# RetNet retention and a gated feed-forward: group 3 begun inside the first block, weights' exponents one part ahead

## The chip, the cores and the metric

One core of a Trainium2 chip runs the whole kernel. The metric is the device time of one execution in microseconds (us); lower is better. The engines named below are PE (TensorE, matrix products), DVE (VectorE), ACT (ScalarE), POOL (GpSimd, here mostly a queue of DMAs) and SP (SyncE, a queue of DMAs). Each engine runs its own instructions in the order in which the program gives them; PE's weight loads run beside its matmuls.

## The reference, cut to what matters

```python
# q, k, v: (4, 8, 768, 64) float32; w_in (512, 2048) and w_out (2048, 512) arrive as float64
for t in range(S):                                   # retention, per batch and head
    state = gamma * state + outer(k[:, :, t], v[:, :, t])
    y[:, :, t] = q[:, :, t] @ state / 8
x = y.transpose(0, 2, 1, 3).reshape(3072, 512)
h = x @ w_in                                         # "hidden"
g = h * erf(softplus(h))
out = (g @ w_out).astype(float32)                    # "project"
```

## The kernel before

**Tokens.** The 3072 tokens are 24 chunks of 128. Chunks 2g and 2g+1 form group g of 256 tokens, so there are 12 groups. Retention is computed chunk by chunk: queries and keys are transposed (`ret_transpose`, or `prepare` with DVE's transposes from chunk 6 on), `begin` makes scores and state updates on PE, `states` masks the scores and adds up the state on DVE, `results` makes the outputs on PE, and `crossed_sums` adds two halves on DVE. The outputs of a group stand in `XC[g]`.

**Weights.** The eight pieces of `w_in` (n = 0 to 7, two of the 16 column tiles `ft` each, 1 MB as float64) are loaded by SP (`load_piece`, L175) and turned into float32 by hand (`conversion`, L204). DVE takes the exponent bits (L216), ACT scales them (L219), and DVE makes the mantissa (L223, L228), puts the sign to the scaled exponent (L230) and multiplies (L242). Pieces 0 to 3 are converted in two half-width parts, the others whole. The call of L219 stands directly behind L216 of the same part, so L230 needs an ACT result that was asked for two or three DVE instructions before. `need("in", ft)` runs conversion steps until tile `ft` is ready. The eight pieces of `w_out` follow later through POOL (`load_quarter`, `convert`).

**First block.** Groups 0 and 1 (the first 512 tokens) meet `w_in` in plain float32: 16 steps, one for each `ft`, each 16 PE instructions (`hidden_of`, L642) and one eviction by ACT (`put_hidden`, L650) into a tile of two that `ps_h` has. The table `during` says what else is put in after which `ft`: before, the whole retention of group 2 (chunks 4 and 5) stands at ft 5 to 13, the loads of chunks 6 and 7 (`load_pair`, the generator `pair`; 32 DMAs of 32 KB in four steps and then four of 256 KB) at ft 6 to 10, and the first splits of weights at ft 8 to 15.

**Periods.** From group 2 on, weights and tokens are split into three fp32r parts (`split_weights`, `split_x`), and a product is three fp32r products. There are two forms of work. A unit alone (`unit`, L667) takes two column tiles for one group: 24 matmuls of 256 columns. A unit in pairs (`pair_unit`, L709) takes one column tile for two groups: 12 matmuls of 512 columns. `period(g)` lists eight or fewer units, puts `begin` and `results` of the next group's chunks between them (`joined`), and the DVE and ACT work beside them. One unit alone of group 2 (n = 7) runs in plain float32 (L679), since its weights aren't split yet. Before, 18 units are alone: eight of group 2, five of group 3, one of group 4 and four of group 11. `put` evicts a unit's two accumulators with one ACT and one DVE instruction (`together`, L296 and L297) and stores the hidden values to DRAM.

**End.** After the periods the hidden values are read back, gated and projected (`project`, L889).

Of the kernel before, what the change touches and what calls it, by code (L numbers as in the profile page):

```python
# [13 lines left out]
F32 = mybir.dt.float32  # L14
# [35 lines left out]
def kernel(  # L50
# [24 lines left out]
    FIRST = 4  # L75
# [25 lines left out]
    HID = {g: scratch.tile([P, n_ft, GT], F32, name=f"hid{g}") for g in (*range(FIRST + 1), NG - 1)}  # L101
# [72 lines left out]
    def load_piece(n, part=None):  # L174

        if n not in RAW:
            if n % 4 < 2:
                RAW[n] = b8("raw", [2 * d_model], I64)
            else:
                raw = ring.tile([P, 3 * d_model], I64, name="raw", tag=f"x{n % 4 - 2}")  # L180
                RAW[n] = raw[:, : 2 * d_model]
        f = slice(2 * P) if part is None else slice(part * P, (part + 1) * P)
        each = 1 if part is None else 2
        for g in range(0, n_k, each):
            nc.sync.dma_start(
                RAW[n].rearrange("p (g f) -> p g f", g=n_k)[:, g : g + each, f],
                w_in[g * P : (g + each) * P, n * 2 * P : (n + 1) * 2 * P].rearrange(
                    "(g p) f -> p g f", p=P
                )[:, :, f],
            )  # L190
# [11 lines left out]
    behind = []  # L202

    def conversion(n):  # L204

        WF[n] = b4("w", [2, 2, 2 * P])
        POWER[n] = b4("power", [2, 2, 2 * P])
        for part in range(2) if n < 4 else (None,):  # L210
            f = slice(2 * P) if part is None else slice(part * P, (part + 1) * P)
            words = RAW[n].bitcast(U32).rearrange("p (h a b w) -> p h a b w", h=2, a=2, w=2)[:, :, :, f]
            to, power = WF[n][..., f], POWER[n][..., f].bitcast(U32)
            number = to.bitcast(U32)
            lo, hi = words[..., 0], words[..., 1]
            nc.vector.tensor_scalar(power, hi, 0x7FF00000, None, op0=ALU.bitwise_and)  # L216
            exponent = partial(nc.scalar.activation, power, power, AF.Relu, bias=below, scale=8.0)
            if n < NPC:
                exponent()  # L219
            else:  # L220
                behind.append(exponent)
            yield
            nc.vector.tensor_scalar(  # L223
                number, hi, 0xFFFFF, 1 << 20, op0=ALU.bitwise_and, op1=ALU.bitwise_or
            )
            if part is None:
                yield
            nc.vector.scalar_tensor_tensor(to, number, 2.0**32, lo, op0=ALU.mult, op1=ALU.add)  # L228
            yield
            nc.vector.scalar_tensor_tensor(  # L230
                power, hi, 1 << 31, power, op0=ALU.bitwise_and, op1=ALU.bitwise_or
            )
            if part != 0:
                del RAW[n]
                if n + 4 < NPC:
                    load_piece(n + 4)
                if n < 2:
                    load(JPC + n)
                    load_values(JPC + n)
            if part is None:  # L240
                yield
            nc.vector.scalar_tensor_tensor(  # L242
                to, to, 2.0**-52, power.bitcast(F32), op0=ALU.mult, op1=ALU.mult,
            )
            if n < NPC:
                done.update(("in", 2 * n + u) for u in (range(2) if part is None else (part,)))
            else:
                nc.gpsimd.dma_start(
                    WOF[n - NPC],
                    WF.pop(n).rearrange("p h a f -> p (h a f)").rearrange("p (f c) -> p f c", f=2),  # L250
                )
            yield

    def weights():


        for n in range(2 * NPC):
            yield from conversion(n)
# [275 lines left out]
    def begin(j, pool=ps_h):  # L534

        SC[j] = [ret_psum(pool) for _ in range(2)]
# [80 lines left out]
    def split_x(j, n=1):  # L617
        g, i = divmod(j, 2)
        if i == 0:
            if g == JPC // 2:  # L620
                X[g] = [b4(f"x_{x}", [HP, GT], F32R) for x in ("hi", "lo", "dif")]
            else:
                if not XR:
                    XR.extend(
                        ring.tile([P, 3, HP, GT], F32R, name=f"x_{x}", tag=f"x{i}")
                        for i, x in enumerate(("hi", "lo", "dif"))
                    )
                X[g] = [x[:, g % 3] for x in XR]
# [27 lines left out]

    def unit(g, n):

        if n in W:
            pool = next(last_turn) if g == NG - 1 else ps_o  # L660
            own = next(turn) if pool is ps_o else None
            names = [f"o{2 * own + i}" if pool is ps_o else "hp" if pool is ps_h else "r" for i in range(2)]
            a, b = (pool.tile([P, 2, GT], F32, name=name) for name in names)
            for to, parts in ((a, (0, 1)), (b, (2,))):
                for u in range(2):
                    for kk, i in itertools.product(range(n_k), parts):
                        nc.tensor.matmul(  # L667
                            to[:, u],
                            W[n][i][:, kk * 2 * P + u * P : kk * 2 * P + (u + 1) * P],
                            X[g][i][:, kk],  # L670
                            start=(u == 0 and kk == 0 and i == parts[0]),
                            stop=(kk == n_k - 1 and i == parts[-1]),
                            skip_group_check=True,
                        )
        else:
            a, b = ps_o.tile([P, 2, GT], F32, name=f"o{2 * next(turn)}"), None
            w = WF[n].rearrange("p h a f -> p (h a) f")
            for u, kk in itertools.product(range(2), range(n_k)):
                nc.tensor.matmul(  # L679
                    a[:, u], w[:, kk, u * P : (u + 1) * P], XC[g][:, kk],  # L680
                    start=(u == 0 and kk == 0), stop=(kk == n_k - 1), skip_group_check=True,
                )

        def put():
            h = b2("h", [2, GT])
            if b is None:
                nc.scalar.copy(h, a)
            else:
                together(h, a, b)
# [8 lines left out]
    def pair_unit(g, ft):  # L698

        pool = next(last_turn) if g == NG - 2 else ps_o  # L700
        own = next(turn) if pool is ps_o else None
        names = [f"o{2 * own + i}" if pool is ps_o else "hp" if pool is ps_h else "r" for i in range(2)]
        a, b = (pool.tile([P, 2, GT], F32, name=name) for name in names)
# [13 lines left out]
        def put():  # L717
            h = b2("h", [2, GT])
            together(h, a, b)
            if g < FIRST:  # L720
                for of in (g, g + 1):
                    nc.gpsimd.dma_start(HID[of][:, ft], h[:, place_of(g, of)])
            else:
                nc.gpsimd.dma_start(HID2[g][:, ft % 8], h)  # L724
# [52 lines left out]

    def steps(s, n=1):
# [8 lines left out]
        5: [(Q_, a), (V_, a)],  # L787
        6: [(T, a, None, ("o2", "o3")), (steps, pair, 2)],
        7: [(begin, a, ps_r), (steps, pair, 2)],
        8: [(states, a), (Q_, b), (V_, b), (split_weights, 0), (steps, pair, 2)],  # L790
        9: [(results, a, ("o0", "o1")), (T, b, None, ("o2", "o3")), (steps, pair, 2)],
        10: [(crossed_sums, a), (begin, b, ps_r), (steps, pair), (block_scales,)],
        11: [(states, b), (split_x, a)],
        12: [(results, b, ("o0", "o1"))],
        13: [(crossed_sums, b), (split_x, b), (split_weights, 1)],
        14: [(split_weights, 2), (steps, prep, 2)],
        15: [(split_weights, 3), (steps, prep, 3)],
    }
    for ft in range(n_ft):
# [4 lines left out]
        need("in", min(ft + 2, n_ft - 1))  # L804
# [9 lines left out]
    def load_hidden(n):  # L814
# [5 lines left out]
        of = g if g % 2 == i // 2 else g - 1  # L820
# [95 lines left out]

    def period(g, prep, next_prep):
# [3 lines left out]
        if g == G2:  # L921
            units = [one(g, n) for n in (0, 7, 1, 2, 3, 4, 5, 6)]
            return units, joined(3, 5, g), {
                1: [(split_weights, 4)],
                2: [(split_weights, 5)],
                3: [(states, a), (states, b)],
                4: [(split_weights, 6)],
# [3 lines left out]
            }, range(8)  # L931
        if g == G2 + 1:
            units = [one(g, n) for n in range(5)]
            return units, joined(1, 3, g), {
                0: [(steps, prep)],
                1: [(states, a), (states, b)],
                2: [(split_weights, 7)],
                3: [(crossed_sums, a), (crossed_sums, b), (split_x, a, 2)],
# [141 lines left out]
```

## Time and profile before

| | |
|---|---|
| median of 3 runs | 617.8 us (616.19 to 619.2) |
| the profiled execution's own time | 616.22 us |
| its span, first to last instruction | 614.4 us |
| PE busy | 606.4 us, 99% |
| DVE, ACT, POOL busy | 461.1, 379.1, 104.2 us |
| granted TensorE clock | 1.000 |
| chain that ended last | PE 96% |

The profiled execution is one of the shorter ones: it lies 1.6 us under the median. Start times below are microseconds from the start of the span.

### The profile page before, as it was taken

What the parts mean: (1) busy time and instruction counts of PE and PEld (TensorE: products, weight loads), DVE (VectorE), ACT (ScalarE), POOL (GpSimd) and SP (SyncE); (2) the same over time, 40 slices, a digit from 0 to 9 for tenths busy, and PEclk for the clock granted to TensorE, in tenths of its full rate; (3) what the DMA queues carried; (4) which work ended last, traced back from release to release, by engine and by line L of the source; (5) the groups of instructions that cost most, each with busy time, mean ns of one, the idle gap of its engine ahead of it and who ended that gap; (6) DMA issues with size and microseconds to landing.
All of it is one profiled execution on the core that took longest, in us unless ns stands there. A gap on an engine that the chain in (4) does not pass through costs nothing.

```text
span 614.4 us, 13336 instructions
## 1 busy us (share of the span) xinstructions
PE 606.4 (99%) x5334; PEld 514.0 (84%) x5334; DVE 461.1 (75%) x583; ACT 379.1 (62%) x566; POOL 104.2 (17%) x198
## 2 busy tenths in 40 slices
PE   8999999999999999999999999999999999999997
PEld 7888899998888888888888988888888888888885
DVE  5988897786878779798758978686786768668640
ACT  3333473563544535454487699879789888988910
POOL 1085332213333242321111200000000000000000
PEclk9999999999999999999999999999999999999999
DMA  9999659677889899787645834325324333531301
GB/s 202 326 249 278 150 130 259 172 160 191 234 238 243 217 264 264 211 231 203 231 136 192 302 118 126 133 84 172 103 83 157 104 127 112 171 123 49 104 34 35
DMA packets 175022, 106.29 MB, mean 173 GB/s; under 512 B 140016, under 2 KB 155632, under 8 KB 174960
## 3 DMA queue, kind: packets, MB, share of 16 engines
q1 hardware_dynamic: 162016, 67.53, 43.3%
q0 software_dynamic: 12384, 37.77, 17.6%
q8 instruction: 42, 0.69, 0.5%
q10 hardware_dynamic: 560, 0.14, 0.1%
q14 instruction: 20, 0.16, 0.1%
HBM read 69.75 MB, written 35.65 MB: 172 GB/s over the span
## 4 chain that ended last, share of the span: by engine, by line
PE 96%; DVE 1%; DMA 1%; SPq 1%; issue 0%; ACT 0%; DVEq 0%
PE o L709 26%; PE o L889 21%; PE r L889 11%; PE hp L889 11%; PE hp L642 9%; PE o L667 7%; PE hp L540 1%; PE hp L709 1%; PE r L709 1%; PE r L585 1%; PE r L540 1%; DMA q<-in_q_dram 1%; PE r L596 1%; PE hp L547 1%; PE r L547 1%; PE hp L585 1%
## 5 line engine op out<-in xcount | busy, mean ns | idle before, releaser
L844 DVE TENSOR_TENSOR e<-hid,e 128x1024 f32<-128x1024 f32 x48 | 56.7, 1222 | 62.1 <-ACT e L834 62.1
L296 ACT ACTIVATE h<-o 128x512 f32<-128x512 f32 x73 | 43.1, 593 | 84.1 <-PE o L709 65.8
L709 PE MATMUL o<-x_hi,w_hi 128*128 128x512 f32 x232 | 92.3, 398 | 0.0
L709 PE MATMUL o<-x_lo,w_lo 128*128 128x512 f32 x232 | 90.4, 390 | 0.0
L297 DVE SCALAR_TENSOR_TENSOR h<-o,h 128x512 f32<-128x512 f32 x73 | 49.7, 683 | 31.6 <-ACT h L296 25.3
L709 PE MATMUL o<-x_dif,w_dif 128*128 128x512 f32 x232 | 62.0, 389 | 0.0
L290 DVE SCALAR_TENSOR_TENSOR g_dif<-g_hi,g_lo 128x1024 fp32r<-128x1024 f32 x48 | 58.8, 1225 | 3.3
L288 ACT ACTIVATE g_hi<-e 128x1024 fp32r<-128x1024 f32 x48 | 51.0, 1062 | 13.6 <-DVE e L844 11.6
L289 DVE TENSOR_TENSOR g_lo<-e,g_hi 128x1024 fp32r<-128x1024 f32 x48 | 58.6, 1221 | 0.5
L642 PE MATMUL hp<-xT,w 128*128 128x256 f32 x256 | 56.9, 381 | 0.0
L642 PEld LDWEIGHTS hp<-xT,w 128*128 128x128 f32 x256 | 48.1, 190 | 6.6
L724 POOL DMA_DIRECT2D hids<-h x56 | 30.4, 543 | 126.3 <-DVE h L297 126.1
L709 PEld LDWEIGHTS o<-x_hi,w_hi 128*128 128x128 f32 x232 | 43.5, 188 | 9.8
L709 PEld LDWEIGHTS o<-x_dif,w_dif 128*128 128x128 f32 x232 | 43.5, 188 | 9.1
L709 PEld LDWEIGHTS o<-x_lo,w_lo 128*128 128x128 f32 x232 | 43.6, 188 | 8.5
L830 ACT ACTIVATE e<-hid 128x1024 f32<-128x1024 f32 x48 | 48.2, 1052 | 0.3
L834 ACT ACTIVATE e<-e 128x1024 f32<-128x1024 f32 x48 | 48.2, 1052 | 0.3
L889 PE MATMUL o<-w_hi,g_hi 128*128 128x512 f32 x120 | 46.7, 389 | 0.0
L889 PE MATMUL o<-w_lo,g_lo 128*128 128x512 f32 x120 | 46.7, 389 | 0.0
L889 PE MATMUL o<-w_dif,g_dif 128*128 128x512 f32 x120 | 46.7, 389 | 0.0
L524 ACT ACTIVATE v<-v,kq_s 128x64 f32<-128x64 f32 x144 | 36.2, 336 | 11.2 <-DMA v<-in_v_dram 11.2
L830 ACT ACT_TABLE_LOAD x24 | 30.8, 1283 | 1.5 <-DMA hid<-hid 1.1
(194 smaller groups left out, 1326.6 us busy)
## 6 DMA issues: line engine op xcount, KB each, us to landing
hids<-h POOLq DMA_DIRECT2D x56, 256.0 KB, 3.6
hid<-hids SPq DMA_DIRECT2D x28, 512.0 KB, 4.6
hid<-hid SPq DMA_DIRECT2D x20, 512.0 KB, 5.2
raw<-in_moe_w_in_dram SPq DMA_DIRECT2D x32, 256.0 KB, 5.7
raw<-in_moe_w_out_dram POOLq DMA_DIRECT2D x32, 256.0 KB, 4.9
v<-in_v_dram SPq DMA_DIRECT2D x24, 256.0 KB, 5.3
out_dram<-y SPq DMA_DIRECT2D x23, 256.0 KB, 2.1
hid<-h POOLq DMA_DIRECT2D x44, 128.0 KB, 3.5
```

The costliest lines, as they stand in the source:

```text
L288: nc.scalar.activation(hi, x, AF.Copy, scale=KEEP)
L289: nc.vector.tensor_tensor(lo, x, hi.bitcast(F32), op=ALU.subtract)
L290: nc.vector.scalar_tensor_tensor(dif, hi.bitcast(F32), Z, lo.bitcast(F32), op0=ALU.mult, op1=ALU.subtract)
L296: nc.scalar.activation(to, a, AF.Copy, scale=1 + 1 / Z)
L297: nc.vector.scalar_tensor_tensor(to, b, -1 / Z, to, op0=ALU.mult, op1=ALU.add)
L642: nc.tensor.matmul(HP_[ft][:, g], w[:, kk, ft % 2 * P : (ft % 2 + 1) * P], XC[g][:, kk], start=(kk == 0), stop=(kk == n_k - 1),)
L667: nc.tensor.matmul(to[:, u], W[n][i][:, kk * 2 * P + u * P : kk * 2 * P + (u + 1) * P], X[g][i][:, kk], start=(u == 0 and kk == 0 and i == ...
L709: nc.tensor.matmul(to, W[n][i][:, kk * 2 * P + u * P : kk * 2 * P + (u + 1) * P], XR[i][:, at, kk], start=(kk == 0 and i == parts[0]), sto ...
L830: nc.scalar.activation(E[n], HID_[n], AF.Softplus)
L834: nc.scalar.activation(E[n], E[n], AF.Erf)
L844: nc.vector.tensor_tensor(E[n], HID_.pop(n), E[n], op=ALU.mult)
L889: nc.tensor.matmul(Y[g][t][x // 2], G[n][x][:, f, t * P : (t + 1) * P], W_OUT[ft // 2][x][:, ft % 2 * d_model : (ft % 2 + 1) * d_model], s ...
```

## The change

It has five parts.

1. The retention of chunks 4 and 5 is put at ft 2 to 10 of the first block instead of 5 to 13. Its queries and values are scaled by 16 small ACT instructions for each chunk (`scale_early`) instead of two DVE instructions.
2. `begin` and `states` of chunks 6 and 7 (group 3) are put behind ft 14. The loads of chunks 6 and 7 move from ft 6 to 10 to ft 2 to 4, and `prepare` from ft 14 and 15 to ft 11 to 13.
3. Period 2 has four units alone, periods 3 to 11 have eight units in pairs each, and group 11 keeps four units alone. Eight units are alone instead of 18, and the plain float32 form of `unit` is gone.
4. L216 and L219 of a part are issued inside the conversion of the part before it, behind that part's L228 (`exponents`, `ahead`), for all parts from the second half of piece 0 on. `need` looks one tile further from ft 4 on.
5. Buffers: pieces 2, 3 and 4 use the three `ring` buffers, the others the two of `wide`. Pieces 4, 5, 6 and 7 are asked for when pieces 0, 1, 2 and 5 are converted (piece 7: when piece 3 was, before). The loads and conversions of `w_out` are placed anew over the periods.

```diff
@@ load_piece
-            if n % 4 < 2:
-                RAW[n] = b8("raw", [2 * d_model], I64)
+            if 2 <= n < 5:
+                raw = ring.tile([P, 3 * d_model], I64, name="raw", tag=f"x{n - 2}")
+                RAW[n] = raw[:, : 2 * d_model]
...
+    NEXT = {0: 4, 1: 5, 2: 6, 5: 7}
...
+    def exponents(n, part):
+
+        _, _, hi, power = views(n, part)
+        nc.vector.tensor_scalar(power, hi, 0x7FF00000, None, op0=ALU.bitwise_and)
+        ready = partial(nc.scalar.activation, power, power, AF.Relu, bias=below, scale=8.0)
+        if n < NPC:
+            ready()
+        else:
+            behind.append(ready)
+
+    def conversion(n, part, ahead):
+
...
+        nc.vector.tensor_scalar(
+            number, hi, 0xFFFFF, 1 << 20, op0=ALU.bitwise_and, op1=ALU.bitwise_or
+        )
+        if part is None:
             yield
...
+        nc.vector.scalar_tensor_tensor(to, number, 2.0**32, lo, op0=ALU.mult, op1=ALU.add)
+        if ahead:
+            exponents(*ahead)
+        yield
+        nc.vector.scalar_tensor_tensor(
+            power, hi, 1 << 31, power, op0=ALU.bitwise_and, op1=ALU.bitwise_or
+        )
+        if part != 0:
+            del RAW[n]
+            if n in NEXT:
+                load_piece(NEXT[n])
...
+    def weights():
+
+        parts = [(n, part) for n in range(2 * NPC) for part in (range(2) if n < 4 else (None,))]
+        for i, (n, part) in enumerate(parts):
+            if n >= NPC or i < 2:
+                exponents(n, part)
                 yield
...
+            yield from conversion(n, part, parts[i + 1] if 0 < i and n < NPC - 1 else ())
...
+    def scale_early(j):
+        q = QN[j].rearrange("p (c g) d -> p c g d", c=2)
+        for i, h in itertools.product((1, 0), range(H)):
+            by, x = kq_s[:, j % NC, i, h : h + 1], q[:, h % 2, h // 2] if i else V[j][:, h]
+            nc.scalar.activation(x, x, AF.Copy, scale=by)
...
     during = {
         1: [(load_block_scales,)],
-        5: [(Q_, a), (V_, a)],
-        6: [(T, a, None, ("o2", "o3")), (steps, pair, 2)],
-        7: [(begin, a, ps_r), (steps, pair, 2)],
-        8: [(states, a), (Q_, b), (V_, b), (split_weights, 0), (steps, pair, 2)],
-        9: [(results, a, ("o0", "o1")), (T, b, None, ("o2", "o3")), (steps, pair, 2)],
-        10: [(crossed_sums, a), (begin, b, ps_r), (steps, pair), (block_scales,)],
-        11: [(states, b), (split_x, a)],
-        12: [(results, b, ("o0", "o1"))],
-        13: [(crossed_sums, b), (split_x, b), (split_weights, 1)],
-        14: [(split_weights, 2), (steps, prep, 2)],
-        15: [(split_weights, 3), (steps, prep, 3)],
+        2: [(scale_early, a), (steps, pair, 2)],
+        3: [(T, a, None, ("o2", "o3")), (steps, pair, 2)],
+        4: [(begin, a, ps_r), (steps, pair, 2)],
+        5: [(states, a), (scale_early, b), (steps, pair, 2)],
+        6: [(results, a, ("o0", "o1")), (T, b, None, ("o2", "o3")), (steps, pair), (block_scales,)],
+        7: [(crossed_sums, a), (begin, b, ps_r), (split_weights, 0)],
+        8: [(states, b), (split_weights, 1)],
+        9: [(results, b, ("o0", "o1"))],
+        10: [(crossed_sums, b), (split_x, a, 2)],
+        11: [(steps, prep, 3)],
+        12: [(split_weights, 2), (steps, prep, 1)],
+        13: [(steps, prep, 1)],
+        14: [(begin, a + 2, ps_r), (begin, b + 2, None, ("o2", "o3")), (split_weights, 3), (states, a + 2), (states, b + 2)],
     }
...
-        need("in", min(ft + 2, n_ft - 1))
+        need("in", min(ft + 2 + (ft > 3), n_ft - 1))
...
         if g == G2:
-            units = [one(g, n) for n in (0, 7, 1, 2, 3, 4, 5, 6)]
-            return units, joined(3, 5, g), {
...
+            units = [one(g, n) for n in range(NPC // 2)]
+            return units, {0: [(results, a), (results, b, None, ps_h)]}, {
+                0: [(crossed_sums, a), (crossed_sums, b)],
+                1: [(split_x, a, 2)],
+                2: [(split_weights, 4)],
+                3: [(steps, next_prep, 4)],
+            }, range(4)
+        if g < NG:
+            units = [two(g - 1, ft) for ft in range(8 * (g % 2), 8 * (g % 2) + 8)]
...
-        return [one(NG - 1, n) for n in range(4, NPC)], {}, {
+        return [one(NG - 1, n) for n in range(NPC // 2)], {}, {
```

## The prediction

> **What bounds the kernel now.** I read the shares of busy time first, then the chain that ended last, then PE's starts one after another.
>
> ```profile
> PE 606.4 (99%) x5334; PEld 514.0 (84%) x5334; DVE 461.1 (75%) x583; ACT 379.1 (62%) x566; POOL 104.2 (17%) x198
> ```
>
> The chain that ended last, in order of time (start, length, what):
>
> ```profile
> 22.12 1.92 PE hp L642 x8
> ...
> 24.64 1.02 PE o L478 x16
> ...
> 86.70 2.87 PE o L667 x24
> 89.57 3.46 PE o L679 x16
> ...
> 105.68 11.71 PE o L667 x96
> ...
> 136.52 0.69 PE hp L540 x32
> ...
> 157.62 5.47 PE o L709 x24
> ...
> 332.03 5.44 PE o L709 x24
> ```
>
> From 22 us on PE never rests, but for some 0.4 us ahead of the `begin` at 136.52. So the change can win only PE work, and it loses by every wait that it brings to PE after 20 us. Which engine comes next in the first block (26 to 86 us) is told by the busy time by stretch (the stretch, its length, then busy us and instructions of PE, PEld, DVE, ACT and POOL):
>
> ```profile
> 26.00:46.00 20.00, 20.00 (x98) 17.59 (x93) 18.10 (x34) 7.96 (x14) 12.41 (x22) 1.00 1.05 282
> 62.00:86.00 24.00, 24.00 (x242) 20.83 (x233) 21.50 (x31) 13.01 (x25) 8.66 (x17) 1.00 0.66 146
> ```
>
> DVE is busy for 90% there: its order counts.
>
> **Part 1, PE work.** By the diff eight units stay alone, so ten change. Nine fp32r units at 2.87 us become pairs at 2.72 (5.44 for two): 9 x 0.15 = 1.35. The plain float32 one (3.46) saves 0.74. The 0.4 at 136.5 goes too, as loads of keys get a longer period. To take in what lies at the switches, I compare whole stretches. Before: from the block's end at 86.70 to the `begin` of period 5 at 163.08 is 76.4. After: `results` 1.82 (103.86 to 105.68), four units 11.7, two pairs 5.5, two periods of eight pairs at 26.05 to 26.33 (`begin` at 163.08, 189.13 and 215.46), and the `begin` put into the block, 2.03 plus some 0.15 for a switch: 73.2 to 73.9. Gain 2.5 to 3.2; I take **-3.1**, since the units' own prices and the gone stall alone give 2.5, and the float32 switches go too.
>
> The Trainium skill (TensorE: Matmul & The Clock Gate, Back-to-back issue gap) gives N/2.4 + 2.5 ns for a matmul of N columns, an estimate of 109 ns for 256 and 216 for 512. By it a unit alone is 2.62 and a pair 2.59, nine changes win 0.3, and the sum is 1.1 later. The rows show 2.87 and 2.72, and they decide.
>
> **Part 2, exponents one part ahead, at the start.** At the second half of piece 0 the new order is L223, L228, then L216 of piece 1, and only then V of chunk 3 (L419). DVE before:
>
> ```profile
> 22.99 0.69 DVE L228 SCALAR_TENSOR_TENSOR w<-w,raw 128x512 f32<-128x512 uint32 x1
> 23.60 0.68 DVE L419 TENSOR_TENSOR v<-v,kq_s 128x512 f32<-128x512 f32 x1
> ...
> 26.51 0.42 DVE L216 TENSOR_SCALAR power<-raw 128x512 uint32<-128x512 uint32 x1
> ```
>
> The L216 that stood at 26.51 is asked for at 23.60. It reads all of piece 1, whose fourth and last DMA is this one, from the view of source line 185, narrowed to its issue:
>
> ```profile
> L185 SPq DMA_DIRECT2D raw<-in_moe_w_in_dram x1: 430/430/430, 19.3 to 19.3; - x1
> ...
> DMA to landing us min/median/max: 5.7/5.7/5.7
> ```
>
> It lands at 19.3 + 5.7 = 25.0. So L216 waits 1.4 and takes 0.34, and L419 ends at 26.0 instead of 24.3. Queued behind are L230 and L242 of piece 0, and PE waits for both: L478 at 24.57 needs V, so it starts at some 26.1: **+1.55**, as PE has no pause later. Were the landing 1 us earlier or later, so is this term: 0.5 to 2.5.
>
> **Part 3, the block on DVE and ACT.** Gone from DVE: four scalings at 0.6 and ACT waits of 0.33, 0.35, 0.64, 1.73 and 0.80 ahead of L230, 6.3 in all. Added: `states` of two chunks, 2 x 1.45. The scalings become 2 x 3.92 on ACT (16 instructions took 3.92 at 84.73), busy for 40% to 54% there. The first ends near 39.6 by ACT's queue, the eviction of ft 2 behind it at 40.1, and PE wants that buffer at 40.5. That is covered by 0.4; past it each us late is one on PE.
>
> The Trainium skill (ScalarE: Activation LUTs, Rules for kernel authors) says to multiply on VectorE, not ScalarE. By it these 2.4 us would stay on DVE, and the sum below would be up to 2.4 later. Here DVE is the fuller engine, so I side with the change.
>
> **Part 4, pieces 6 and 7 come later.** SP before, in order:
>
> ```profile
> 37.92 3.69 SPq L140 DMA_DIRECT2D v<-in_v_dram  x1
> 41.71 4.90 SPq L185 DMA_DIRECT2D raw<-in_moe_w_in_dram  x8
> ...
> 58.60 1.93 SPq L151 DMA_DIRECT2D kb<-in_k_dram  x4
> 60.57 1.98 SPq L151 DMA_DIRECT2D qb<-in_q_dram  x4
> 62.59 3.11 SPq L151 DMA_DIRECT2D kb<-in_k_dram  x4
> 65.75 1.97 SPq L151 DMA_DIRECT2D qb<-in_q_dram  x4
> 67.83 1.01 SPq L140 DMA_DIRECT2D v<-in_v_dram  x2
> 68.94 2.11 SPq L162 DMA_DIRECT2D kn<-in_k_dram  x2
> ```
>
> The eight DMAs at 41.71 are pieces 6 and 7. After, 16 of the small DMAs stand ahead of piece 6 (16 take 9.1 at 58.60; 11.2 at 47.43 under load), then 16 more, four large ones (3.2) and piece 7. From 41.7: piece 6 is issued at 50.8 to 53, and lands last 5 to 6 later: 57.5 (56 to 59). Piece 7 is issued from 64 to 66, and lands behind V and K (which took 4.7 to land): 71.5 (68 to 74.5). L216 of piece 7 now stands inside the conversion of piece 6, so that conversion ends only behind piece 7's landing.
>
> DVE's walk with durations of before (whole piece 4.87: L216 0.60, L223 0.73, L228 1.15, L230 1.26, L242 1.14): L216 of piece 6 at 57.5, piece 5 done 60.5; crossed sums 0.4, split 2.4, `states` 1.45, split 2.4, L223 and L228 of piece 6: 69.0. Wait to 71.5; piece 6 done 74.5; `split_x` with ACT's 1.06 ahead of it 78.4; piece 7 done 82.7; `prepare` 3.4: 86.1; two splits 90.9; `states` 92.4 and 93.8. PE's side: ft 2 starts at 32.7 (26.05, three products of 1.73, and the 1.55), a step takes 3.46, and two each of transposes 0.9, `begin` 1.1 and `results` 1.1 lie between; so ft 12 wants piece 6 at 73.5 (late by 1.0), ft 14 then wants piece 7 at 81.4 (late by 1.3), and the second `results` its state at some 92.9 (late by 0.5). Sum **+2.9**. With piece 7 at 68.5 it is about 0.3; each us past 71.5 adds one, to 5.9 at 74.5. These waits hang on piece 7's landing, not on PE: were the wait of part 2 shorter, they would be longer by as much.
>
> Hidden elsewhere: in period 3 DVE has some 21.7 of work in 26; keys of chunks 8 and 10 have more time; w_out's quarters move, and their waits stand on DVE, behind evictions that have a unit (2.72) to spare.
>
> **Sum.** -3.1 + 1.55 + 2.9 = **+1.35**. The profiled execution's own 616.2 (1.8 over its span) becomes 617.6; it lies 1.6 under the median of 617.8, which becomes **619.1**. 0.5% is 3.1 us, about what a measurement of this kernel can tell from no change.
>
> **Rivals.** *The loads are in time.* If piece 1 lands by 23.6 and piece 7 by some 67, only PE's gain is left: 617.8 - 3.1 = 614.7, at best 614.3. For it speaks that DMA is less busy from 62 us on (0.66); against it the landing at 25.0, which stands in the trace. Chance 0.14. *Slower: piece 7 decides.* If it lands late, conversions, splits and states come late by as much: at 74.5 they cost 5.9 instead of 2.9, so +4.35: 622.2. It decides from 73.3 on, where the sum reaches +3.1. For it: SP's long issues behind V and K (3.69 at 37.92), and a DVE that has no rest to make it up; against it the emptier DMA. Chance 0.26. *ACT's scaling holds an eviction.* If V of chunk 4 lands 2 us past its 36.8, PE waits 1.6 at ft 4; but part 4's waits shrink by as much, and the time stays 619. It counts only past some 4.5 us, and I give it no chance of its own. My case has 0.60.
>
> **Numbers.** My case ranges from 616.5 (piece 7 at 68.5) to 620.9 (at 73.3). With part of both rivals, 8 in 10 lie in 614.8 to 622.3. Faster by over 0.5%: the better half of the first rival and a little, 0.09. Slower by over 0.5%: the second, 0.26. Within 0.5%: 0.65.
>
> **What would show it.** Right: of 18 units alone 8 are left and the float32 one is gone; from the block's end to the `begin` of period 5 PE takes 71 to 72; DVE waits for a raw DMA near 23.6 and near 69, PE starts L478 at 26. Wrong: no wait for raw on DVE, a PE pause at ft 4 to 8, or a gap in periods 3 to 5, where I see none.

## The result, and the profile after

The changed kernel takes 625.24 us (median of 6 runs, 624.74 to 627.33) beside 618.02 us (616.19 to 620.41) for the kernel before on the same chip: ratio 1.0123, 95% interval 1.0095 to 1.0151. It is 7.2 us slower, outside the predicted range of 614.8 to 622.3. The profiled execution took 625.19 us over a span of 623.2 us, 8.8 us more than the span before. Of the named cases it is the one that ends slower, piece 7's landing, and the loss is larger than that case had it.

Line numbers after: `unit` L683, `pair_unit` L710, the block's products L655, their evictions L663, the exponents L220 (DVE, before L216) and L223 (ACT, before L219), the sign L243, V's scaling L435, and the product that waits for it L494. The page's busy times and its row of granted clock by slice:

```profile
PE 607.1 (97%) x5222; PEld 508.5 (82%) x5222; DVE 459.1 (74%) x578; ACT 386.2 (62%) x597; POOL 101.9 (16%) x192
...
PEclk9999989999999999999999999999999999999999
```

PE has fewer instructions and a longer busy time, and its clock falls in one slice of 40, near 80 us. What stops it shows in the waits of PE between 20 and 100 us (what waited, for whom, us in total, times, longest):

```profile
PE hp L655 <- ACT h L663: 7.1, 1, 7.1
PE o L494 <- DVE v L435: 2.1, 1, 2.1
```

Both waits lead to raw weights. DVE's timeline (start, length, instruction, and in brackets the idle time ahead and who ended it):

```profile
25.34 0.43 DVE L220 TENSOR_SCALAR power<-raw 128x512 uint32<-128x512 uint32 x1 [1.97 <-DMA raw<-in_moe_w_in_dram]
...
75.48 0.69 DVE L220 TENSOR_SCALAR power<-raw 128x1024 uint32<-128x1024 uint32 x1 [9.65 <-DMA qb<-in_q_dram]
```

ACT's timeline:

```profile
76.21 1.15 ACT L223 ACTIVATE power<-power,below 128x1024 uint32<-128x1024 uint32 x1 [12.44 <-DVE power L220]
77.26 0.63 ACT L620 COPY xT<-o 128x256 f32<-128x256 f32 x2
77.78 0.60 ACT L663 COPY h<-hp 128x512 f32<-128x512 f32 x1
```

DVE reached piece 7's exponents at 65.8 and stood 9.65 us. ACT had the second half of the same step in its queue (L223) and stood 12.44 us, and behind it, in program order, stood the evictions (L663) of products that PE had long finished. PE had no accumulator left and stopped at 71.3, at ft 11, until the eviction at 77.78; it was back at 78.43. (DVE's wait is put down to a `qb` DMA at the end of SP's queue; piece 7's last transfer landed at 75.36, by its own record.) SP's timeline shows why piece 7 was so late:

```profile
46.08 3.32 SPq L188 DMA_DIRECT2D raw<-in_moe_w_in_dram  x4
49.44 2.09 SPq L154 DMA_DIRECT2D kb<-in_k_dram  x4
...
62.09 1.94 SPq L154 DMA_DIRECT2D qb<-in_q_dram  x4
64.14 1.02 SPq L143 DMA_DIRECT2D v<-in_v_dram  x2
65.20 2.60 SPq L165 DMA_DIRECT2D kn<-in_k_dram  x2
67.90 3.42 SPq L188 DMA_DIRECT2D raw<-in_moe_w_in_dram  x4
```

The row at 46.08 is piece 6, the last one piece 7. SP goes from row to row with gaps of 0.5 us at most, so piece 7 is late by its place in this queue: between the two SP issues 24 small loads of chunks 6 and 7 (14.6 us) and four of 256 KB (3.6 us). Before, the two pieces stood side by side at 41.71. The last loss is in the busy time by stretch (stretch, its length, busy us and instructions of PE, PEld, DVE, ACT and POOL, granted clock, DMA share, GB/s):

```profile
71.00:78.40 7.40, 0.29 (x2) 0.00 (x0) 2.89 (x3) 2.17 (x4) 0.00 (x0) 0.85 0.69 173
78.40:82.00 3.60, 3.57 (x8) 2.87 (x9) 2.39 (x5) 1.53 (x2) 2.14 (x4) 0.50 0.62 145
82.00:87.00 5.00, 5.00 (x22) 4.35 (x21) 4.93 (x6) 2.54 (x7) 1.07 (x2) 0.89 0.62 139
```

Behind the pause the clock is at half, from 76.24 to 83.07; PE works from 78.43 on, so 4.64 us of work run at half speed: 2.3 us lost. The chain that ended last has the gain of part 1:

```profile
78.43 16.36 PE hp L655 x64
...
102.34 11.71 PE o L683 x96
114.05 5.47 PE o L710 x24
```

Four units alone take 11.71 us, two in pairs 5.47. By PE's starts the stretch from the block's end (100.39) to the `begin` of period 5 (172.00) is 71.6 us, and `begin` in the block adds 2.0 to 2.1: 73.7 for 76.4 to 76.7 before (from 86.70 by the chain, from 86.35 by PE's starts). Account of the span: start wait +2.1, stop +7.1, half clock +2.3, work of PE -2.9, together +8.6 of the 8.8 measured. From that `begin` to the end the two traces take the same time, 451.2 and 451.4 us, and after 100 us PE has no wait in the view of waits: the later periods and the moved loads of `w_out` have no part in the loss.

### The profile page after: what moved, and what is told of

Same layout as the page of the kernel before. It is cut to its first block, busy times and chain, and to the rows that moved or that the text cites. A ratio compares the mean times of both kernels' runs of the same rounds, so it can differ in the third digit from the quotient of the medians.

```text
span 623.2 us, 13124 instructions
## 1 busy us (share of the span) xinstructions
PE 607.1 (97%) x5222; PEld 508.5 (82%) x5222; DVE 459.1 (74%) x578; ACT 386.2 (62%) x597; POOL 101.9 (16%) x192
## 4 chain that ended last, share of the span: by engine, by line
PE 87%; SPq 6%; DMA 4%; DVE 1%; issue 1%; ACT 0%; DVEq 0%
PE o L710 30%; PE o L895 21%; PE hp L895 10%; PE r L895 10%; PE hp L655 3%; PE o L683 3%; SPq L188 2%; SPq L154 2%; DMA raw<-in_moe_w_in_dram 2%; SPq L136 1%; PE hp L556 1%; PE hp L710 1%; PE r L710 1%; DMA kb<-in_k_dram 1%; DMA v<-in_v_dram 1%; PE r L601 1%
## 5 line engine op out<-in xcount | busy, mean ns | idle before, releaser
L710 PE MATMUL o<-x_hi,w_hi 128*128 128x512 f32 x272 | 108.1, 397 | 0.0
L710 PE MATMUL o<-x_lo,w_lo 128*128 128x512 f32 x272 | 106.0, 390 | 0.0
L850 DVE TENSOR_TENSOR e<-hid,e 128x1024 f32<-128x1024 f32 x48 | 56.7, 1222 | 61.6 <-ACT e L840 61.6
L710 PE MATMUL o<-x_dif,w_dif 128*128 128x512 f32 x272 | 72.7, 389 | 0.0
L721 POOL DMA_DIRECT2D hids<-h x72 | 39.0, 542 | 170.1 <-DVE h L313 164.3
L655 PE MATMUL hp<-xT,w 128*128 128x256 f32 x256 | 59.7, 392 | 7.1 <-ACT h L663 7.1
L655 PEld LDWEIGHTS hp<-xT,w 128*128 128x128 f32 x256 | 49.6, 196 | 14.7 <-ACT h L663 7.5
L710 PEld LDWEIGHTS o<-x_hi,w_hi 128*128 128x128 f32 x272 | 51.0, 188 | 11.5
L710 PEld LDWEIGHTS o<-x_dif,w_dif 128*128 128x128 f32 x272 | 51.1, 188 | 10.7
L710 PEld LDWEIGHTS o<-x_lo,w_lo 128*128 128x128 f32 x272 | 51.1, 188 | 10.1
```

Of the source, the lines that this page charges most:

```text
L655: nc.tensor.matmul(HP_[ft][:, g], w[:, kk, ft % 2 * P : (ft % 2 + 1) * P], XC[g][:, kk], start=(kk == 0), stop=(kk == n_k - 1),)
L710: nc.tensor.matmul(to, W[n][i][:, kk * 2 * P + u * P : kk * 2 * P + (u + 1) * P], XR[i][:, at, kk], start=(kk == 0 and i == parts[0]), sto ...
L850: nc.vector.tensor_tensor(E[n], HID_.pop(n), E[n], op=ALU.mult)
```

## The experiments

The question was which edit's wait costs the 7.2 us, and whether the late landing, the order of DVE's queue or the halved clock stands behind it. Kernels with edited lines above have their lines one to five further down (L656 for L655 and so on). Three groups of four ran on three occasions, each beside its own runs of the kernel before (medians 616.66, 618.93 and 616.76 us; in the second its runs went from 615.95 to 625.22), so ratios are compared rather than times. The shortest runs of the kernel before agree on the three occasions (616.09, 615.95 and 615.95), so the ratios of the second, from e5_load7 to e8_warm, may come out up to 0.3% too favourable beside those of the others; shortest runs are given where this matters.

### Exponents at their own place: piece 7, piece 1, both

```diff
-            if n >= NPC or i < 2:
+        early = [i for i in range(2, len(parts)) if parts[i][0] < NPC and (...)]
+            if i not in early:
                 exponents(n, part)
                 yield
-            yield from conversion(n, part, parts[i + 1] if 0 < i and n < NPC - 1 else ())
+            yield from conversion(n, part, parts[i + 1] if i + 1 in early else ())
# e1_own7: ... is  parts[i][0] != 7
# e2_own1: ... is  i > 2          (piece 1's first half is part 2)
# e3_own17: both
```

**e1_own7.**

> The changed kernel, but the exponents of piece 7 (DVE's and ACT's instruction) stand at piece 7's own conversion again; all other parts keep theirs one part ahead. Theory (order): piece 7 lands at 75.4 in the changed kernel, and what costs PE's 7.3 us and the half clock behind it is that its exponents are asked for inside piece 6's conversion, so that DVE (9.65) and ACT (12.4) wait with piece 6 and two evictions behind them. Then DVE should wait some 3 us for piece 7 at its own place, PE should not rest between ft 9 and ft 14, the clock stay at 1.0, and the time be 625.2 - 9.8 = 615.4 (614.5 to 617). Rival (lateness): piece 7 comes too late whatever the order, and ft 14 waits instead of ft 11: some 4 us less than now, 621.

Measured 617.21 us, ratio 1.0008 (0.9983 to 1.0033). PE does not stop in the block, though piece 7 lands no sooner (77.93). So the late landing alone does not make the stop of 7 us; it takes piece 7's exponents asked for inside piece 6's conversion as well. At their own place DVE waits 2.33 us for the piece, and nothing that PE wants just then is behind it. The time stayed 1.8 us over the expected 615.4; in that profile the wait at the first chunk was 3.3 us, with 3.4 us of half clock behind it. The five of the ten runs with a mean clock of 0.999 or more took 615.7 to 616.7 us, inside the expected range.

**e2_own1.**

> The changed kernel, but the exponents of piece 1's first half stand at their own place again (V of chunk 3 no longer waits behind them). PE's wait at 24 us (2.1 us) should go. Theory (piece 7 decides): the end of the block hangs on piece 7's landing, which SP's queue sets, so PE only waits longer at ft 11: time 625.2 within 0.7. Rival (the waits add): 625.2 - 2.1 = 623.1.

Measured 626.07 us, 1.0141 (1.0107 to 1.0176), within 0.2 us of the theory's range and far from the rival: the start wait goes, and the stop in the block grows to 8.7 us. In this execution most of that growth is a later landing (76.72 for 75.36). PE reached the stop only 0.2 us sooner, since its first product of the block began 0.8 us later and an eviction at ft 4 held it for 0.9.

**e3_own17.**

> Both edits: exponents of piece 1's first half and of piece 7 at their own places. Theory (order): only PE's gain of 2.9 us in periods 2 to 5 is left, 618.0 - 2.9 = 615.1 at most, and counted from the changed kernel 625.2 - 9.8 - 2.1 = 613.3; so 613.3 to 615.1. Rival (DVE is the bound at the end of the block): without the 2.1 us of lateness PE runs into DVE's chain there, and the time stays that of the run with piece 7 alone.

Measured 617.06 us, 1.0000 (0.9986 to 1.0014): no better than with piece 7 alone, as the rival had it. PE's timeline shows two new waits:

```profile
40.82 3.72 PE L656 MATMUL hp<-xT,w 128*128 128x256 f32 x16 [1.23 <-ACT h L664]
...
79.94 7.17 PE L656 MATMUL hp<-xT,w 128*128 128x256 f32 x32 [1.79 <-ACT h L664]
```

At 40.8 the eviction stands behind `scale_early` on ACT; at 79.9 it stands behind piece 7's L223, for DVE reaches that L220 at 72.5 and still waits 5.08 us for the landing. The theory was too hopeful: what the start gave was eaten by the same late piece and by ACT.

### ACT's half of piece 7 alone at its own place

```diff
+        if n == NPC - 1:
+            held.append(ready)      # called at the head of piece 7's conversion
-        if n < NPC:
+        elif n < NPC:
             ready()
```

**e4_act7.**

> The changed kernel; DVE's part of piece 7's exponents stays one part ahead, ACT's part stands at piece 7's own conversion. Tells ACT's queue from DVE's. Theory (both queues count): DVE still waits 9.65 us, but ft 9 and 10 are evicted in time; PE rests only ahead of ft 12, from 74.6 to 78.6, and some 1.4 at ft 14: 5.4 us, and the half clock may come or not (2.5): 620.8 to 623.3. Rival (DVE's wait is all): PE gets no further, 625.2.

Measured 625.29 us, 1.0125 (1.0089 to 1.0160): the time is the rival's, the trace is the theory's. PE got one step further and stopped ahead of ft 12 for 4.3 us (expected 4.0), not at ft 11 for 7.1. But the start wait was 3.3 us in that profile instead of 2.1, with 3.4 us of half clock (1.7 us lost), and this took back the 2.8 us won; so in that execution the time agrees with the rival by chance; the other three runs have no trace. Another 6.8 us of half clock came with the stop. ACT waited 8.65 us ahead of the split of group 2's tokens (L309), which needs `crossed_sums` of DVE (L636), and these stood behind piece 7's exponents (L221), which waited 8.09 us. Freeing ACT's queue alone does not do: what ACT needs next stands behind the same wait on DVE.

### Piece 7's load ahead of the other loads

```diff
-        4: [(begin, a, ps_r), (steps, pair, 2)],
-        5: [(states, a), (scale_early, b), (steps, pair, 2)],
-        6: [..., (steps, pair), (block_scales,)],
-        7: [..., (split_weights, 0)],   8: [..., (split_weights, 1)],   9: [(results, b, ("o0", "o1"))],
+        4: [(begin, a, ps_r)],
+        5: [(states, a), (scale_early, b)],
+        6: [..., (block_scales,)],
+        7: [..., (split_weights, 0), (steps, pair, 2)],
+        8: [..., (split_weights, 1), (steps, pair, 2)],
+        9: [(results, b, ("o0", "o1")), (steps, pair)],
```

**e5_load7.**

> The changed kernel with the small Q/K loads of chunks 6 and 7 that stood ahead of piece 7 on SyncE's queue issued later: 16 of the 24 and the V and K loads go behind ft 7. Theory (SP's order sets piece 7's landing, and all of the wait in the block hangs on it): piece 7 lands 16 x 0.6 + 3.7 = 13.4 us sooner, near 62, ahead of DVE's reaching its exponents (65.8); no wait of DVE or ScalarE for it, no stop of PE near ft 11, no halved clock behind it: 625.2 - 7.3 - 2.4 = 615.5 us. Rival (chunks 6 and 7's late loads or DVE's own order take the wait's place): a stop of some us near ft 14 or in the first units of the next period, 618 to 622.

Measured 616.16 us, 0.9947 (0.9919 to 0.9974): by moving loads alone the loss is gone, and the kernel comes out faster than the kernel before, by 0.5% beside that occasion's runs and by 0.3% from shortest run to shortest run (614.16 and 615.95). Piece 7 was issued from 56.7 and landed at 64.34; DVE took its exponents at 65.90 without a wait. SP's row of piece 7, and all waits of PE from 20 to 100 us:

```profile
56.71 1.78 SPq L188 DMA_DIRECT2D raw<-in_moe_w_in_dram  x4
...
PE o L494 <- DVE v L435: 1.0, 1, 1.0
PE r L455 <- ACT kqT L449: 0.6, 1, 0.6
```

The stop is gone, the clock is 1.000 throughout, and nothing took the wait's place in the block. SP's order made piece 7 late. With `e1_own7` this shows both halves of the cause: the stop needs the late landing and the exponents asked for ahead, and goes when either is taken away. (The profiled spans, 614.3 and 614.4 before, hardly differ: this execution began its first product 0.7 us later and waited 1.0 us at the first chunk, and took 0.6 us longer from the `begin` of period 5 on.)

**e6_load7_own1** (the same, and piece 1's first half at its own place).

> As the run with piece 7's load ahead, and the exponents of piece 1's first half left at their own conversion. Theory: both waits for raw weights are gone, 615.5 less the 2.1 of the first chunk, plus up to 1.2 for the eviction at ft 4 that then meets scale_early on ScalarE: 613.3 to 614.6. Rival (PE is already held by something else there): as the run with piece 7's load ahead alone.

Measured 615.02 us, 0.9939 (0.9909 to 0.9968). The start wait is gone and PE waits 1.4 us at ft 4 for an eviction, as named; its profile's span is 1.0 us shorter than that of e5_load7, but the ranges of the two kernels' runs overlap, so the times do not tell them apart.

```diff
# e7_late_scale: e6_load7_own1, and
-        2: [(scale_early, a), ...],   5: [(states, a), (scale_early, b)],
+        3: [(scale_early, a), ...],   6: [(scale_early, b), ...],
```

**e7_late_scale.**

> As the run before it, with scale_early(a) moved from ft 2 to ft 3 and scale_early(b) from ft 5 to ft 6. Theory (the stop of PE near ft 4, 1.2 to 1.5 us in the two runs with piece 1's exponents at their own place, is the eviction queued behind scale_early on ScalarE): that stop goes, 0.9 to 1.5 us faster than the run before it, near 613. Rival: the scaling is then late for the first products of period 4 in the block, and the begin waits as long: no change or slower.

Measured 614.75 us, 0.9918 (0.9888 to 0.9947). In the trace the wait at ft 4 is gone, and from the block's first product to the first unit alone PE takes 69.2 us instead of 70.4. The span did not shrink (613.4 and 613.3), since this execution began its first product 0.7 us later and lost 0.5 us in the later periods. That ACT's scaling held the eviction is shown; that it is worth 1 us in the median is not.

### The pause filled with idle products

```diff
         need("in", ft)
+        if ft == 11:
+            warm = ps_o.tile([P, P], F32, name="o2")
+            for _ in range(30):
+                nc.tensor.matmul(warm, ident, ident, start=True, stop=True)
```

**e8_warm.**

> The changed kernel with 30 extra 128x128 matmuls of the identity on PE ahead of ft 11, inside the 7.3 us in which it waits. They work out nothing that is used. Theory (the halved granted clock follows from PE's pause): the clock stays near 1.0 behind the wait, PE resumes at the same 78.4 and the 2.4 us of slow matmuls go: 622.8 us. Rival (the clock falls for another reason): 625.2 or a little more.

Measured 623.88 us, 1.0088 (1.0060 to 1.0115), beside 1.0123 (1.0095 to 1.0151) of the changed kernel: 0.35%, or 2.2 us, though the two intervals meet. The stretches:

```profile
71.00:78.40 7.40, 7.40 (x62) 7.22 (x61) 2.56 (x3) 1.86 (x4) 0.00 (x0) 1.00 0.70 184
78.40:82.00 3.60, 3.60 (x21) 3.27 (x21) 2.39 (x5) 1.83 (x3) 1.88 (x4) 1.00 0.61 137
```

Piece 7 was no earlier for DVE (75.81), but the clock stays at 1.00, and the mean clock of all eight runs is 0.997 or more, for 0.991 to 0.994 in the six of the changed kernel. So the half clock comes from the pause. Its price, 2.2 us by the ratios, is near the 2.3 worked out above.

### The exponents in the kernel before

The `views`, `exponents` and `conversion` of the change are put into the kernel before, which keeps its own tables, groups and `load_piece(n + 4)`.

**e9_base_ahead.**

> The kernel before with one part of the change alone: exponents asked for one part ahead; retention, loads and groups as before. Theory (the exponents cost a wait only where the piece asked for lands late): piece 1's wait of 2.1 at the first chunk comes in, while piece 7, which lands at 53.4 in the kernel before, makes no wait: ratio 1.0035 to the kernel before, 620.1 for 618.0. Rival (asking ahead itself puts DVE's and ScalarE's queues behind and stops PE in the block as well): 1.008 or more.

Measured 618.59 us for 616.76, ratio 1.0036 (1.0013 to 1.0059): the theory's 1.0035. PE's timeline:

```profile
26.36 1.09 PE L490 MATMUL o<-am,v 128*64 128x128 f32 x16 [1.43 <-DVE v L431]
```

So the exponents cost 1.4 us at the first chunk by themselves (1.8 by the medians), and the rest needs the late piece 7. The execution that was profiled was the longest of twelve (623.2 us): V landed late for one period, PE waited 3.0 us for an ACT eviction behind it, and the clock followed (PE alone: stretch, length, busy us, instructions, clock, DMA share, GB/s):

```profile
262.00:270.80 8.80, 5.84 (x27) 1.00 1.00 209
270.80:274.20 3.40, 3.40 (x10) 0.50 0.60 136
```

### No exponents ahead, and the scaling on VectorE

```diff
# e10_own_all: e7_late_scale with an empty list of early parts
# e11_dve_scale: e7_late_scale, and in scale_early
-        for i, h in itertools.product((1, 0), range(H)):
...
-            nc.scalar.activation(x, x, AF.Copy, scale=by)          # 16 times
+        by = kq_s[:, j % NC, 1].rearrange("p (g c) -> p c g", c=2)[..., None]
+        nc.vector.tensor_tensor(q, q, by.to_broadcast([P, 2, HP, D]), op=ALU.mult)
+        scale_v(j)
```

**e10_own_all.**

> As the run with the late scaling (piece 7's load ahead, piece 1 at its own place), with no exponents ahead at all. Theory (once the pieces are there in time, asking ahead hides the 0.7 to 1.7 us in which DVE waits for ScalarE's exponents, and DVE has slack): the same within 0.5 us as that run. Rival (DVE is the engine that the products of the late ft wait for, so that waiting for ScalarE in each piece adds up): 1 to 3 us slower than that run.

Measured 615.36 us, 0.9971 (0.9956 to 0.9986). DVE waits 2.84 us once for ACT's exponents, and PE then waits 1.0 us at 52 us for a state that DVE makes late; e7_late_scale has no such wait. From the block's first product to the first unit alone PE takes 69.9 us, for 69.2 in e7_late_scale. So the traces put asking ahead at some 0.7 us where the weights are in time, between theory and rival. The times can't settle it: the two kernels ran on different occasions, and are 0.6 us apart by medians, 0.8 by shortest runs (614.58 and 613.78) and over 3 by ratios.

**e11_dve_scale.**

> As the run with the late scaling, with Q and V of chunks 4 and 5 multiplied on VectorE (4 instructions of 0.6 to 0.7) and not on ScalarE (32 of 0.1 to 0.25). Theory (DVE is the fuller engine, and the products of ft 4 and on wait for its conversions): up to 2.4 us slower than that run. Rival (with the raw weights there in time DVE has slack in the block, and VectorE's are the shorter instructions): the same or up to 0.5 us faster.

Measured 614.10 us, 0.9957 (0.9934 to 0.9980), span 612.4, the shortest of all; from 20 to 100 us PE waits once, 0.6 us at the very start, and from the block's first product to the first unit alone it takes 68.8 us, for 69.2 in e7_late_scale. So in the trace PE does not feel the 2.4 us more on DVE, and the theory is refuted there. By ratios this kernel would be 2.4 us slower than e7_late_scale; this is the size of the difference between the two occasions, and the shortest runs agree (613.59 and 613.78). The rule of the Trainium skill (ScalarE: Activation LUTs, Rules for kernel authors), against which the prediction sided with the change, holds in this trace at least as no loss.

### V and K of chunks 6 and 7 alone behind piece 7

```diff
-        6: [..., (steps, pair), (block_scales,)],
-        7: [..., (split_weights, 0)],
+        6: [..., (block_scales,)],
+        7: [..., (split_weights, 0), (steps, pair)],
```

**e12_vk_late.**

> The changed kernel with V's and K's four loads of chunks 6 and 7 alone put behind piece 7's on SyncE's queue (3.7 us of issue): piece 7 then lands near 71.7, where the prediction had it (71.5). By the prediction's own walk behind such a landing (waits of 1.0, 1.3 and 0.5 at ft 12, ft 14 and the results): 619.1 to 619.5. By the account of the changed kernel's trace (PE stops at ft 11 for an eviction behind ScalarE's waiting exponent, and comes back 3.1 us after the landing): the stop is 7.3 - 3.7 = 3.6 us, and 621.5 with a halved clock behind it, 619.1 without.

Measured 619.31 us, 1.0024 (1.0004 to 1.0044). SP's timeline and the waits of PE:

```profile
62.05 1.93 SPq L154 DMA_DIRECT2D qb<-in_q_dram  x4
64.09 1.83 SPq L188 DMA_DIRECT2D raw<-in_moe_w_in_dram  x4
66.02 1.33 SPq L143 DMA_DIRECT2D v<-in_v_dram  x2
```

```profile
PE hp L655 <- ACT h L663: 2.4, 1, 2.4
PE o L494 <- DVE v L435: 1.5, 1, 1.5
```

Piece 7 is issued at 64.09 instead of 67.90 and lands at 70.56 instead of 75.36, 4.8 us sooner; the stop is 4.7 us shorter. In both traces PE is back 3.07 us after the landing, as the account of the changed kernel's trace had it. With `e5_load7` that makes three points: landing 75.4, stop 7.1; 70.6, 2.4; 64.3, none. The median is the prediction's own number for a landing near 71, but not by its walk: one stop of 2.4 us for an eviction at ft 11 and 3.4 us at half clock (1.7 us lost), 4.1 together, where the walk had about 2.0 for 70.6 (2.9 for 71.5, and some one less for each us). So the agreement of the median is luck.

## Why the prediction was wrong, by its steps

**Part 1** was right: -2.9 in the trace for -3.1, 71.6 us for the stretch named as 71 to 72. The row of 2.87 us for a unit alone held (11.71 for four).

**Part 2** was right in its mechanism and near in size: 2.1 in the profile after, 1.4 to 1.5 in e9_base_ahead and e12_vk_late, 1.0 in e5_load7, 2.4 in e8_warm, 3.3 in e1_own7 and e4_act7, for 1.55 (0.5 to 2.5). It hangs on piece 1's landing, which differs between executions: at 25.2 to 25.3 in those with a wait of 1.0 to 2.1, at 26.5 to 26.6 in those with 2.4 and 3.3.

**Part 3's** rival, ACT's scaling holding an eviction, came once the start wait was gone and PE reached ft 4 sooner (1.2 and 1.4 us in e3_own17 and e6_load7_own1, where ACT also waited 1.3 us for V of chunk 4); in the changed kernel the start wait hid it. The step that took DVE to be too full for the four scalings was wrong where the loads are in time (e11_dve_scale).

**Part 4** failed, at three points.

- *The landing.* Predicted 71.5, measured 75.4. The walk along SP put piece 7's issue at 64 to 66 by adding 16 small DMAs (9.1) and four large ones (3.2) to the start of piece 6's issue (by these numbers 63.1 to 65.3). Piece 6's own issue was left out: half of the row of 4.90, and 3.3 measured. SP came to piece 7 at 67.90, and the last landing was 7.5 after that instead of some 6.5. I also took a step of `pair` for eight DMAs; it is four, so only eight stood ahead of piece 6, which landed at 53.8 instead of 57.5, and DVE came to piece 7's exponents sooner and stood longer.
- *Who is queued behind the wait.* The walk followed DVE alone. ACT's L223 stands in the program behind L220, with the evictions of ft 9 and 10 behind it, so PE stopped at ft 11 in one piece, and not at ft 12, ft 14 and the results. By the prediction's own rule the landing alone makes 2.9 + 3.9 = 6.8 us; the stop was 7.1, near in size by another path. (The walk's waits of 1.0, 1.3 and 0.5 make 2.8, and by its own times of 92.9 and 93.8 the last is 0.9.)
- *The clock.* The 2.3 us behind the pause had no term at all.

Together: landing 3.9, clock 2.3, start 0.5, stop's form 0.3 and PE work 0.2 are 7.2 of the 7.4 us between the predicted +1.35 and the measured +8.8 of the span. The rival "piece 7 decides" named the mechanism, and its time (622.2 at 74.5) had the same missing terms; its chance of 0.26 was too small, since the rows already gave an issue at 65.6 to 69.8 (41.7, 32 small DMAs at 0.57 to 0.70, piece 6's 2.45, four large ones 3.2) and so, 6.5 later, a landing from 72 on.

## What to carry to other kernels

When a change moves loads, add up the whole queue from its last known start to the load in question, large issues too, and only then ask when it lands. For every instruction that may wait, list what is queued behind it on each engine that its result passes through: here a conversion moved by a few lines put two evictions on another engine behind a DMA. When a kernel turns out slower, look first whether another order of its loads gives the gain back: e5_load7 differs from the changed kernel in that alone, and takes it from 1.2% slower to 0.5% faster than the kernel before; e7_late_scale and e11_dve_scale are 0.8% and 0.4% faster. From shortest run to shortest run all three are 0.3% to 0.4% faster.

## What the runs showed of the hardware

A pause of PE costs more than its length. After pauses of 3.0 (e9_base_ahead) and 3.3 us (e1_own7, e4_act7) the granted clock fell to 0.5 for 3.4 us, from 0.6 to 1.1 us after PE was back. With pauses of 4.3, 7.1 and 8.7 us (e4_act7, the changed kernel, e2_own1) it was at half for 6.8 us, and the fall came while PE still waited. With 2.2 us and less it stayed at 1.0. At 2.4 us it went both ways: half in e12_vk_late, full in e8_warm's wait at the first chunk. Thirty idle products put into the pause of 7.1 us kept the clock up and, by the ratios, won 2.2 us.

What decides is where the pause falls. In every one of the 14 traces the clock changes only at whole steps of 3.413 us, counted from its first record (in the changed kernel 21 steps after it, at 76.24, and two more, at 83.07). PE's idle time within each step, by the trace's modelled ends of matmuls, tells the cases apart. At full clock, every step with 2.20 us of idle time or more ended in half clock (2.20 in e12_vk_late, 2.3 and 2.4 in e1_own7 and e4_act7, 2.78 in e9_base_ahead), and no step with 1.93 or less did. The pause of e12_vk_late lay almost whole in one step; that of e8_warm, as long, was cut into 1.70 and 0.74 by the end of a step. At half clock, steps with 2.00 and 2.19 us of idle time (e4_act7, the changed kernel) did not bring the clock back, and those with 0.5 or less did.

The Trainium skill (TensorE: Matmul & The Clock Gate, Part 1: The HAM clock gate) states that the clock halves after an idle window of about 3.4 us, that as long a busy one restores it, and that the windows run freely. The steps of 3.413 us and the stretches of one and two of them agree. But the pause itself was shorter than such a window in four of these cases (2.4, 3.0 and twice 3.3 us), and by the steps above 2.2 us of idle time in one window was enough, and 1.9 was not.
